# The row sums D of an attention backward as one column of products, read by VectorE as a scalar per row

## The chip, the cores and the metric

The kernel runs on one core of a Trainium2 chip. The metric is the device time of one execution in microseconds (us); the median of several runs is given. TensorE multiplies (PE in the profile's lines, its weight loads PEld), VectorE (DVE), ScalarE (ACT) and GpSimd (POOL) work element by element, and SyncE (SP) issues DMA transfers.

## The reference

Forward, a block with conditioned layer norms, a segment-recurrent attention with a memory of 8 rows, and a gated MLP; the kernel returns its output and the gradients of eleven inputs for a given `grad_out`. The attention, with 64 segments of 32 rows, 32 heads of 128 and 40 positions in each segment (8 of memory, 32 of the segment):

```
for s in range(64):
    h = concatenate([mem, x[s * 32:(s + 1) * 32]])            # 40 rows of 512
    q, k, v = h @ Wq, h @ Wk, h @ Wv                          # per head
    p = softmax(where(mask, q @ k.T * scale, -1e9))           # 40 x 40 per head
    o = (p @ v) @ Wo
    mem, out[s] = o[:8], o[8:]
```

Its backward runs from the last segment to the first, because `mem` ties each segment to the one behind it. For each head, with dO the gradient of `p @ v`:

```
dV = P.T @ dO
dP = dO @ V.T
D  = rowsum(dO * O)
dS = scale * P * (dP - D)
dQ = dS @ K;  dK = dS.T @ Q
dh = dQ @ Wq.T + dK @ Wk.T + dV @ Wv.T
```

## The kernel before

The program has stages: setup and forward attention (to about 930 us of the span), the MLP forward and backward (to about 1456 us), the backward of the attention (`phase4`, to about 2420 us), and the weight gradients of the attention (`phase5`). The change lies in `phase4` alone, a loop of 64 steps, one for each segment.

The 32 heads are laid out as 11 groups of three heads (3 x 40 = 120 rows, in columns of 128). Most steps work on all 11 groups in three batches of 4, 4 and 3 groups (`NP = 3`, `PG = 4`), one batch to a PSUM bank, since a batch is 4 x 128 float32. One step does, in the order in which it is written:

- `col_pass`: the products dO = dy Wo^T; `turn` transposes them into `dOT`; copies also make `dOst`, dO by rows.
- `grad_mm("dVT", ...)`: products for dV transposed (tile `g_ps`, line 1890); `prod(pi)`: VectorE multiplies `OT` by `dOT` in place (line 1849); `dp(pi)`: the products dP into `dp_ps` (line 1867).
- `ds(pi)`: for each group one product with a matrix of minus ones (`negones`) that adds -D to all 120 columns of dP in the same bank (line 1875). Then one VectorE instruction for the batch takes (dP - D) times `scale` times `Pst` into `dS` (line 1877).
- `dht(dVT, WvT, 0)` and `1`: the heads of dV in the products for dh (`col_mm`, line 215, four at a time in 32 columns each; 24 heads, then the last 8 later).
- `gv2`: the last batch for dV transposed; `gr0`, `gr1`, `gr2`: three batches for dV by rows, copied by `rv_out` into `rv_rows` (shown as `rows_x`), the first by ScalarE, the others by VectorE.
- `dstt(pi)`: TensorE transposes `dS` into `tps` (line 1807), a copy makes `dST`: batches 0 and 2 by ScalarE, 1 by VectorE.
- `gks`: products for dK (line 1890, `g_ps<-dS,Qst`), copied by `grad_out` into `dKT`: batch 0 by ScalarE, 1 and 2 by VectorE. Then `gq`: products for dQ (`g_ps<-dST,Kst`), copied by ScalarE into `dQT`. Behind the last copy of each, SyncE issues a transposing DMA, and GpSimd later stores the rows.
- `dht` for the 32 heads of dK and the last 8 of dV; `fold_split` takes that sum; `dht_pairs` multiplies dQ; `sum_pair` adds, and ScalarE puts the memory rows of the result into the next segment's `dyT`.

Copies go through one helper, `evac` (lines 61 and 63). At the end of the loop `pin` fixes the program's order on every engine as it is written, so nothing is reordered. Some steps have extras: every fourth step VectorE copies half of a tile `RBd` ahead of its dS instructions, another fourth ScalarE copies the other half, and in some 14 steps a small transpose from another sum (`dh_b`) stands in the place of this step's own, which comes later.

PSUM tiles of the loop with the tag `p` share a pool of six banks:

```
psp = self.psp = self.ps_ctx.enter_context(tc.tile_pool(name="p4ps", bufs=6, space=PSUM, reuse_waits="tile"))
```

When a tile is asked for, the pool picks one of the banks whose last tile has been given up in the program's order. The first product into the new tile waits for the last instruction that read the old one. Which bank a tile gets is settled when the program is built, and can change when the instructions before it do.

Of the kernel before, what the change touches and what calls it, by code (L numbers as in the profile page):

```python
# [9 lines left out]
AF = mybir.ActivationFunctionType  # L10
ALU = mybir.AluOpType
# [29 lines left out]
class K:  # L41
# [1631 lines left out]
    def phase4(self):  # L1673
        nc, tc, cfg, io = self.nc, self.tc, self.cfg, self.io
        D, DC, H, E, L, M, T, G, NS = cfg.D, cfg.DC, cfg.H, cfg.E, cfg.L, cfg.M, cfg.T, cfg.G, cfg.NS
        GW = 128
# [4 lines left out]
        with self.p4_ctx as ctx:  # L1681
            WqT, WkT, WvT, WoT, negones = self.WqT, self.WkT, self.WvT, self.WoT, self.negones
# [9 lines left out]
            PG = 4  # L1692
# [28 lines left out]
            def part3(t, pi):  # L1721
                return t[:, pi * PW:min((pi + 1) * PW, G * GW)].rearrange("p (g x) -> p g x", x=GW)
# [79 lines left out]
            def transposes_part(src, pi, w=GW, m=128):  # L1802
                ps = ps_b16("tps")
                n = min(PG, G - pi * PG)
                for j in range(n):
                    g = pi * PG + j
                    nc.tensor.transpose(ps[:, j, 0:m], src[0:m, g * w:g * w + GW], self.ident[0:m, 0:m])  # L1807
                return ps[:, 0:n, 0:m]
# [22 lines left out]
            for s in reversed(range(NS)):  # L1831
# [11 lines left out]
                VT, OT, Pst, Kst, Qst = ld["VT"], ld["OT"], ld["Pst"], Kst_t, Qst_t  # L1843
                dS, dST, dOst = dSs[0], dSTs[0], dOst_t
                dVT, dKT, dQT = dXTs["dVT"][0], dXTs["dKT"][0], dXTs["dQT"][0]
# [24 lines left out]
                def ds(pi):  # L1870
                    ps = dps[pi]
                    n = min(PG, G - pi * PG)
                    for j in range(n):
                        g = pi * PG + j
                        nc.tensor.matmul(ps[:, j, 0:120], lhsT=OT[:, g * GW:(g + 1) * GW], rhs=negones[:, 0:120],  # L1875
                                         start=False, stop=True, skip_group_check=True)
                    nc.vector.scalar_tensor_tensor(out=part3(dS, pi)[:, :, 0:120], in0=ps[:, 0:n, 0:120],  # L1877
                                                   scalar=cfg.scale, in1=part3(Pst, pi)[:, :, 0:120],
                                                   op0=ALU.mult, op1=ALU.mult)

                def grad_part(nm, lh, rh, xt, pi, eng):
                    grad_out(nm, xt, pi, eng, grad_mm(nm, lh, rh, pi))

                def grad_mm(nm, lh, rh, pi):
                    ps = ps_f32("g_ps")
                    n = min(PG, G - pi * PG)
                    for j in range(n):
                        g = pi * PG + j
                        w = GW if nm == "dV" else 120
                        nc.tensor.matmul(ps[:, j, 0:w], lhsT=lh[:, g * GW:(g + 1) * GW], rhs=rh[:, g * GW:g * GW + w],  # L1890
                                         start=True, stop=True)
                    return ps

                def grad_out(nm, xt, pi, eng, ps):
                    self.evac(eng, part3(xt, pi)[:, :, 0:120], ps[:, 0:min(PG, G - pi * PG), 0:120])
                    if pi == NP - 1 and nm != "dVT":
                        rows = rxp.tile([128, G, 128], BF16, name="rows_x")
                        nc.sync.dma_start(rows[:], xt[:, :], transpose=True)
                        dram = {"dKT": self.DKR, "dQT": self.DQR}[nm][s]
                        row_stores.append(lambda: nc.gpsimd.dma_start(dram, rows[:]))  # L1900
# [3 lines left out]
                def rv_out(pi, eng, ps):  # L1904
                    n = min(PG, G - pi * PG)
                    self.evac(eng, rv_rows[:, pi * PG:pi * PG + n, :], ps[:, 0:n, :])

                def dstt(pi):
                    ps = transposes_part(dS, pi, m=120)
                    self.evac("dve" if pi == 1 else "act", part3(dST, pi)[:, :, 0:120], ps)  # L1910
# [4 lines left out]
                def dht(X, WT, pi):  # L1915
                    if dh_ps[0] is None:
                        dh_ps[0] = psb.tile([128, 512], F32, name="dh_ps", tag="dh")
                    for h in range(pi * PG * 3, min(H, (pi + 1) * PG * 3)):
                        off = (h // 3) * GW + (h % 3) * 32
                        self.col_mm(dh_ps[0], X[:, off:off + 32], WT[:, h, :], n_dh[0], 2 * H)  # L1920
                        n_dh[0] += 1
# [35 lines left out]
                prod(2)  # L1957
                dp(2)
                grad_out("dVT", dVT, 0, "act", gv0)
                if b_done:  # L1960
                    b_done()
                dost(2)
                grad_out("dVT", dVT, 1, "act", gv1)
                ds(0)
                ds(1)
                ds(2)
                self.pop_later()
                dht(dVT, WvT, 0)
# [3 lines left out]
                gr1 = grad_mm("dV", Pst, dOst, 1)  # L1972
# [11 lines left out]
                    self.dO_tails(s - 1, RBds[((s - 1) // 4) % 2])  # L1984
                grad_out("dVT", dVT, 2, "dve", gv2)
                rv_out(0, "act", gr0)
                rv_out(1, "dve", gr1)
                dstt(0)
                dstt(1)
                dstt(2)  # L1990
                rv_out(2, "dve", gr2)
                row_stores.append(lambda s=s, rows=rv_rows: nc.gpsimd.dma_start(self.DVR[s], rows[:]))
# [5 lines left out]
                for pi in range(NP):  # L1998
# [2 lines left out]
                        load_rows(Kst_t, self.KST, s - 1)  # L2001
                    grad_out("dQT", dQT, pi, "act", gq)
                split = tail.split()
                for pi in range(NP):
                    dht(dKT, WkT, pi)
                dht(dVT, WvT, 2)
                parts = self.fold_split(sb2, dh_ps[0], "dh", dST)
                pair = self.split_pair(sb2, dht_pairs(dQT, WqT), "dh")
                tail.collect(s % nseg_t, [dVT, dKT, dQT])
# [7 lines left out]
                g = s // 4  # L2017
# [469 lines left out]
```

## Time and profile before

| What | us |
|---|---|
| median of 3 runs | 2976.55 |
| lowest and highest of them | 2974.73 to 2981.98 |
| profiled execution, its own time | 2976.49 |
| span of that execution | 2974.4 |
| a plain step of the backward loop | 14.5 |
| TensorE busy in the loop, 1456 to 2420 us | 951.87 of 964 |
| VectorE, ScalarE, GpSimd busy there | 577.77, 499.66, 447.31 |

The span is what the profile's lines add up in; the execution's own time has 2.1 us more around it. Products are pipelined and their ends are modelled, so that a busy TensorE may still have small waits between starts. In the lines of instruction groups the numbers are busy us, mean ns of one, and then the idle time of the engine just before them with what ended most of it. In the timeline each line is start, length, engine, line, operation, tiles (out<-in), shape and count, and instructions of one kind that follow each other are one line.

### The profile page before, as it was taken

The numbers are of one execution on the slowest core, as the hardware profiler recorded it, in microseconds if no ns is written. First come the engines' busy times: TensorE is split into PE (matmuls) and PEld (weight loads), VectorE is DVE, ScalarE is ACT, GpSimd is POOL, SyncE is SP. The second block draws the span as 40 slices with busy tenths as digits, with TensorE's granted clock in tenths as the row PEclk, the third lists the DMA queues.
The fourth block names the chain that finished last, engine by engine and source line by source line (L and its number), as shares of the span: only waits on it lengthen the run. The fifth ranks groups of instructions, "written<-read, shape, count | busy, mean of one in ns | idle before, by whom it ended". The sixth has DMA issues, their size and how long they took to land.

```text
span 2974.4 us, 105326 instructions
## 1 busy us (share of the span) xinstructions
PE 2905.7 (98%) x43742; PEld 1816.9 (61%) x43816; DVE 1620.3 (54%) x3683; ACT 1348.0 (45%) x3244; POOL 1233.2 (41%) x2486
## 2 busy tenths in 40 slices
PE   6999999999998999999999999999999999999999
PEld 3666666666665544445677777777777754445545
DVE  5565666656655788733456666666566532850011
ACT  3666666666665544312355555555555520110011
POOL 2555545545545222221344444444444432762111
PEclk9999999999999999999999999999999999999999
DMA  9888898988999899998699999999999997876565
GB/s 308 221 223 220 213 218 229 217 216 224 223 226 267 209 234 229 246 280 274 190 252 256 252 250 252 249 253 247 253 251 252 247 274 246 262 252 191 161 215 171
DMA packets 838066, 703.01 MB, mean 236 GB/s; under 512 B 537698, under 2 KB 710162, under 8 KB 836692
## 3 DMA queue, kind: packets, MB, share of 16 engines
q1 hardware_dynamic: 711972, 485.29, 66.3%
q0 software_dynamic: 54512, 148.63, 15.8%
q10 hardware_dynamic: 71104, 62.34, 6.5%
q8 instruction: 345, 5.65, 0.8%
q14 instruction: 133, 1.09, 0.1%
HBM read 294.99 MB, written 276.35 MB: 192 GB/s over the span
## 4 chain that ended last, share of the span: by engine, by line
PE 89%; DMA 5%; DVE 2%; issue 2%; ACT 1%; SPq 1%; POOL 1%; DVEq 0%; POOLq 0%; ACTq 0%
PE gps L2267 14%; PE pass_ps L257 14%; PE dh_ps L215 8%; PE g_ps L1890 5%; PE pass_ps L675 5%; PE gps5o L2282 4%; PE dhq_ps L223 4%; PE at_ps L223 4%; PE mm L1371 3%; PE gps L1550 3%; PE dh_tps L215 3%; PE turn_ps L880 2%; PE mm L1331 2%; PE mm L1346 2%; PE tps L1807 2%
## 5 line engine op out<-in xcount | busy, mean ns | idle before, releaser
L2267 PE MATMUL gps<-rows,hrows 128*128 128x512 bf16 (+2 forms) x2124 | 413.6, 355 | 1.9
L2267 PEld LDWEIGHTS <-hrows 128*128 128x128 bf16 x2160 | 211.1, 98 | 204.5 <-issue 0.9
L1118 POOL TENSOR_TENSOR Pst<-Pst,rden 120x1408 bf16<-120x1408 bf16 x63 | 159.7, 2535 | 315.1 <-issue 204.0
L63 DVE CAST ot<-gps 128x512 bf16<-128x512 f32 (+3 forms) x76 | 48.2, 634 | 310.8 <-PE gps L2267 229.2
L61 ACT ACTIVATE ot<-gps 128x512 bf16<-128x512 f32 (+3 forms) x75 | 41.2, 549 | 355.0 <-PE gps L2267 228.0
L1935 POOL COPY dOst<-RAd 96x512 bf16<-96x512 bf16 x128 | 75.1, 611 | 297.0 <-DVE RAd L63 297.0
L675 PE MATMUL pass_ps<-Wv,hT 128*32 128x512 bf16 (+2 forms) x2304 | 186.7, 357 | 0.0
L2271 POOL DMA_DIRECT2D out_dram<-ot x104 | 78.5, 755 | 257.6 <-DVE ot L63 133.4
L257 PEld LDWEIGHTS <-hT 128*32 128x32 bf16 x4096 | 117.0, 97 | 96.5 <-issue 6.2
L63 DVE CAST Vst<-pass_ps 96x512 bf16<-96x512 f32 x128 | 87.1, 681 | 106.5 <-ACT RBv L61 103.0
L215 PE MATMUL dh_ps<-WvT,dVT 128*32 128x512 bf16 x2048 | 133.4, 380 | 1.8 <-DVE RBd L63 0.2
L223 PE MATMUL at_ps<-Wo,OT 128*32 128x256 bf16 x4096 | 127.8, 276 | 1.2 <-ACT OT L61 1.0
L675 PE MATMUL pass_ps<-Wv,hb 128*32 128x512 bf16 (+2 forms) x636 | 126.5, 339 | 0.2 <-POOL hb L428 0.2
L257 PE MATMUL pass_ps<-Wk,hT 128*32 128x512 bf16 x2048 | 122.7, 380 | 2.1 <-POOL hT L561 1.1
L257 PE MATMUL pass_ps<-Wq,hT 128*32 128x512 bf16 x2048 | 124.1, 381 | 0.0
L257 PE MATMUL pass_ps<-WoT,dyT 128*32 128x256 bf16 (+1 forms) x3072 | 122.6, 308 | 0.9 <-ACT dyT L2016 0.9
L223 PE MATMUL dhq_ps<-WqT,dQT 128*32 128x256 bf16 x4096 | 122.9, 273 | 0.0
L215 PE MATMUL dh_ps<-WkT,dKT 128*32 128x512 bf16 x2048 | 122.3, 380 | 0.0
L2282 PE MATMUL gps5o<-WoT,rows 128*128 128x512 bf16 x549 | 120.4, 379 | 1.2 <-DMA rows<-OSR 0.6
L223 PEld LDWEIGHTS <-dQT 128*32 128x32 bf16 x4096 | 109.8, 97 | 15.7
L317 DVE TENSOR_TENSOR dST<-dh_ps,dST 128x512 bf16<-128x512 f32 x64 | 44.3, 692 | 130.0 <-ACT dST L316 130.0
L1877 DVE SCALAR_TENSOR_TENSOR dS<-dp_ps,Pst_l 128x480 bf16<-128x480 f32 (+1 forms) x192 | 106.3, 610 | 10.0 <-PE dp_ps L1875 4.1
(475 smaller groups left out, 7038.6 us busy)
## 6 DMA issues: line engine op xcount, KB each, us to landing
OSR<-Ost SPq DMA_DIRECT2D x64, 352.0 KB
OT<-OT SPq DMA_DIRECT2D x64, 352.0 KB
PS<-Pst SPq DMA_DIRECT2D x64, 352.0 KB
Pst_l<-PS SPq DMA_DIRECT2D x64, 352.0 KB
OT_l<-OT SPq DMA_DIRECT2D x64, 352.0 KB
DVR<-rows_x POOLq DMA_DIRECT2D x64, 352.0 KB, 6.3
DKR<-rows_x POOLq DMA_DIRECT2D x64, 352.0 KB, 6.1
DQR<-rows_x POOLq DMA_DIRECT2D x64, 352.0 KB, 3.2
```

What stands on the lines that cost most here:

```text
L63: return nc.vector.tensor_copy(out, in_)
L215: self.nc.tensor.matmul(ps[32 * j:32 * j + 32, :], lhsT=lhsT, rhs=w, start=(n < 4), stop=(n >= total - 4), tile_position=(0, 32 * j))
L223: nc.tensor.matmul(ps[32 * j:32 * j + 32, :], lhsT=x[k], rhs=w[k][:, 256 * d:256 * d + 256], start=(n == 0), stop=(n == total - 1), tile_p ...
L257: self.nc.tensor.matmul(ps[32 * j:32 * j + 32, :], lhsT=lhs(c), rhs=rhs, start=(c == 0), stop=(c == DC - 1), tile_position=(0, 32 * j))
L675: nc.tensor.matmul(ps[32 * j:32 * j + 32, o * E:(o + n) * E], lhsT=lhsT, rhs=wc[:, 3 * a + hl:3 * (a + n - 1) + hl + 1:3, :], start=(c == ...
L1118: nc.gpsimd.tensor_tensor(Pst[0:120, :, :], Pst[0:120, :, :], rden[:, :].unsqueeze(2).to_broadcast([120, G, 128]), op=ALU.mult)
L1371: nc.tensor.matmul(hp[:], lhsT=xT[:, fc, :], rhs=wT[:, fc, :], start=(n == 0), stop=(n == 2 * FC - 1))
L1550: nc.tensor.matmul(ps[:], lhsT=h2r[:, j, c * 128:(c + 1) * 128], rhs=xr[:, j, :], start=(j == 0), stop=(j == NT - 1))
L1877: nc.vector.scalar_tensor_tensor(out=part3(dS, pi)[:, :, 0:120], in0=ps[:, 0:n, 0:120], scalar=cfg.scale, in1=part3(Pst, pi)[:, :, 0:120], ...
L1890: nc.tensor.matmul(ps[:, j, 0:w], lhsT=lh[:, g * GW:(g + 1) * GW], rhs=rh[:, g * GW:g * GW + w], start=True, stop=True)
L2267: nc.tensor.matmul(ps[:, 0:ng * E], lhsT=hrows[:, tp_, c * 128:(c + 1) * 128], rhs=rows[:, tp_, 0:ng * E], start=(tp_ == 0), stop=(tp_ == ...
L2282: nc.tensor.matmul(pss[gg][:], lhsT=rows[:, t, gg * E:(gg + 1) * E], rhs=dyrows[:, t, :], start=(n == 0), stop=(n == NTP - 1))
```

## The change

D is formed once for each row instead of in 120 equal columns. The product with `negones` gets one column, written into column 120 of the group's 128 in dP's bank, which was not used. VectorE's one instruction for a batch becomes one for each group, 11 in a step: it reads that column as a scalar per row, adds it to dP, and multiplies by `Pst`. The factor `scale` leaves it, and stands in the copies of dK and dQ instead, which multiply by a constant.

Two lines also change place: VectorE's copy `rv_out(1)` goes behind the first two `dstt`, and the last 8 heads of dV go ahead of the 32 heads of dK in the products for dh. Instructions on TensorE, ScalarE, GpSimd and the DMA queues are as many as before; VectorE has 8 x 64 = 512 more.

```diff
                     for j in range(n):
                         g = pi * PG + j
-                        nc.tensor.matmul(ps[:, j, 0:120], lhsT=OT[:, g * GW:(g + 1) * GW], rhs=negones[:, 0:120],
+                        nc.tensor.matmul(ps[:, j, 120:121], lhsT=OT[:, g * GW:(g + 1) * GW], rhs=negones[:, 0:1],
                                          start=False, stop=True, skip_group_check=True)
-                    nc.vector.scalar_tensor_tensor(out=part3(dS, pi)[:, :, 0:120], in0=ps[:, 0:n, 0:120],
-                                                   scalar=cfg.scale, in1=part3(Pst, pi)[:, :, 0:120],
-                                                   op0=ALU.mult, op1=ALU.mult)
+                    for j in range(n):
+                        o = (pi * PG + j) * GW
+                        nc.vector.scalar_tensor_tensor(out=dS[:, o:o + 120], in0=ps[:, j, 0:120], scalar=ps[:, j, 120:121],
+                                                       in1=Pst[:, o:o + 120], op0=ALU.add, op1=ALU.mult)
...
                 def grad_out(nm, xt, pi, eng, ps):
-                    self.evac(eng, part3(xt, pi)[:, :, 0:120], ps[:, 0:min(PG, G - pi * PG), 0:120])
+                    dst, src = part3(xt, pi)[:, :, 0:120], ps[:, 0:min(PG, G - pi * PG), 0:120]
+                    if nm == "dVT":
+                        self.evac(eng, dst, src)
+                    elif eng == "act":
+                        nc.scalar.activation(dst, src, AF.Copy, scale=cfg.scale)
+                    else:
+                        nc.vector.tensor_scalar_mul(dst, src, cfg.scale)
                     if pi == NP - 1 and nm != "dVT":
...
                 grad_out("dVT", dVT, 2, "dve", gv2)
                 rv_out(0, "act", gr0)
-                rv_out(1, "dve", gr1)
                 dstt(0)
                 dstt(1)
+                rv_out(1, "dve", gr1)
                 dstt(2)
                 rv_out(2, "dve", gr2)
...
                 split = tail.split()
+                dht(dVT, WvT, 2)
                 for pi in range(NP):
                     dht(dKT, WkT, pi)
-                dht(dVT, WvT, 2)
```

## The prediction

> **What bounds the kernel now.** I read the page first, then the waits, the groups by shape, and the timeline of one step of the backward loop. The profiled execution took 2976.49 us, at the median of the runs shown (2976.55), so sums go against 2976.5; its span is 2974.4, with 2.1 us around it.
>
> ```profile
> PE 2905.7 (98%) x43742; PEld 1816.9 (61%) x43816; DVE 1620.3 (54%) x3683; ACT 1348.0 (45%) x3244; POOL 1233.2 (41%) x2486
> PE 89%; DMA 5%; DVE 2%; issue 2%; ACT 1%; SPq 1%; POOL 1%; DVEq 0%; POOLq 0%; ACTq 0%
> ```
>
> TensorE carries the chain that ended last; VectorE and ScalarE are half idle. So VectorE work counts only where TensorE comes to wait for it. The loop takes about 14.6 us a step, 64 times. The timeline of a plain step (start, length, engine, line, operation, count), other rows left out:
>
> ```profile
> 1905.33 0.98 DVE L1849 TENSOR_TENSOR OT_l<-dOT,OT_l 128x480 bf16<-128x480 bf16 x3
> 1906.04 0.74 PE L1875 MATMUL dp_ps<-negones,OT_l 128*128 128x120 bf16 x11
> 1906.45 1.66 DVE L1877 SCALAR_TENSOR_TENSOR dS<-dp_ps,Pst_l 128x480 bf16<-128x480 f32 x3
> 1906.63 0.56 ACT L61 ACTIVATE dVT<-g_ps 128x480 bf16<-128x480 f32 x1
> 1906.77 1.48 PE L215 MATMUL dh_ps<-WvT,dVT 128*32 128x512 bf16 x24
> 1908.35 0.78 PE L1890 MATMUL g_ps<-dOst,Pst_l 128*128 128x128 bf16 x11
> 1908.77 0.60 ACT L61 ACTIVATE rows_x<-g_ps 128x512 bf16<-128x512 f32 x1 [1.58 <-PE g_ps L1890]
> 1908.96 0.74 PE L1807 MATMUL tps<-ident,dS 120*128 120x120 bf16 x11
> 1909.07 0.68 DVE L63 CAST rows_x<-g_ps 128x512 bf16<-128x512 f32 x1
> 1909.37 0.93 ACT L61 ACTIVATE dST<-tps 128x480 bf16<-128x480 bf16 x2
> 1909.54 0.79 PE L1890 MATMUL g_ps<-dS,Qst 128*128 128x120 bf16 x11
> 1910.16 0.74 PE L1890 MATMUL g_ps<-dST,Kst 128*128 128x120 bf16 x11
> 1910.19 0.58 ACT L61 ACTIVATE dKT<-g_ps 128x480 bf16<-128x480 f32 x1
> 1910.84 1.91 PE L215 MATMUL dh_ps<-WkT,dKT 128*32 128x512 bf16 x32
> ```
>
> From 1908.35 to 1910.84 TensorE runs four blocks of 11 products with almost nothing between them: gr, the transposes of dS, gk, gq. Each block goes in batches of 4, 4, 3, each in one of six rotating PSUM banks. A batch of four lasts 0.21 us, ScalarE's copy of one 0.5 to 0.6. This stretch is smooth only while no batch needs a bank copied out just before.
>
> **The products for D.** Before, 11 products 120 wide start (0.74 - 0.216)/10 = 0.052 us apart. No row shows one column; the nearest is 32 columns, after it the groups of L1877 and scalar operands used below (busy, mean ns):
>
> ```profile
> L242 PE MATMUL dh_ft<-foldsel,dh_hi 128*128 128x32 bf16 x256 | 16.8, 179 | 2.0 <-ACT dh_hi L230 2.0
> L1877 DVE SCALAR_TENSOR_TENSOR dS<-dp_ps,Pst_l 128x480 bf16<-128x480 f32 x128 | 78.2, 653 | 10.0 <-PE dp_ps L1875 4.1
> L1877 DVE SCALAR_TENSOR_TENSOR dS<-dp_ps,Pst_l 128x360 bf16<-128x360 f32 x64 | 33.6, 524 | 0.0
> L1386 DVE SCALAR_TENSOR_TENSOR junk<-dxh,xh 128x512 f32<-128x512 f32 x15 | 10.2, 681 | 0.0
> L1393 DVE SCALAR_TENSOR_TENSOR ta<-dxh,rstd,Wk 128x512 f32<-128x512 f32 x8 | 5.9, 743 | 0.0
> ```
>
> In the timeline four 32-wide products end 0.27 us after the first starts, so they start (0.27 - 0.18)/3 = 0.03 apart. The bounds are 0.052 (nothing saved) and 0.03; I take 0.03, the narrow row: 11 x 0.022 = 0.24 us. Not all of it arrives. The last three products need the last OT*dOT product (L1849, done at 1906.31), so start at 1906.36 rather than 1906.46, 0.05 being the lag from a copy's end to the product waiting for it (below). The dVT heads start at 1906.60, not 1906.77. Their second dozen needs ScalarE's dVT copy, done at 1906.63 + 0.56 = 1907.19; with 0.04 to the weight load and 0.09 to the product that is 1907.32, against 1907.42 now. So TensorE gains 0.10 us in a plain step; 0.02 in the 16 steps where ScalarE also copies half of RBd and dVT is 0.08 later; nothing in some 14 where VectorE copies the other half, for which these heads wait. About 0.06 x 64 = 4 us.
>
> **VectorE.** Three instructions a step become eleven. The rows give (653 - 524)/120 = 1.08 ns per element, so 120 elements cost 653 - 360 x 1.08 = 266 ns; the scalar read per row adds 743 - 681 = 62: 328 ns. Three now take 1.66 us where their lengths add to 1.83, so each overlaps the next by 0.085. Eleven starting d apart end 10 d + 0.33 after the first: d is 0.19 if the scalar is fetched under cover (266 - 85, rounded up), 0.24 with it, 0.33 with no overlap. I take 0.24: 2.7 us against 1.66. Starting at 1906.34 they end at 1909.1, not 1908.1. [...]
>
> **The moved copy.** rv_out(1) (0.68 us, VectorE) goes behind VectorE's dST copy (0.40). VectorE then ends the dST copy at about 1910.05, rv_out(1) at 1910.65, rv_out(2) 1911.1, dKT 1911.7 and 1912.1. Putting the 8 last dVT heads first costs nothing and gives the dKT copies 2 x 0.216 = 0.43 us more room.
>
> **The scale** in the dK and dQ copies: the same instruction with a constant, at the copies' 0.52 to 0.60 us. Bounds nothing to the 62 ns above on each; I take nothing. No DMA is added; those of dK and dQ are issued from the same copies.
>
> **The banks.** Here the sum is decided. In the built program of the changed kernel, in nearly every step, the first batch of dS transposes gets the bank that held the first batch of gr, and so waits for ScalarE's copy of it; before, that bank came from VectorE's last dS instruction, long done. The first gk batch then waits for ScalarE's dST copy of that very transpose batch; before, it waited for the gr copy. The second gq batch waits for ScalarE's dKT copy of the first gk batch (in some 14 steps with one more small transpose, the first gq batch does). So four batches pass through one bank, each behind a ScalarE copy:
> - gr's first batch starts its last product at 1908.52, less 0.10 gained: 1908.42. ScalarE starts 0.25 later (1908.77 now), 0.60: 1909.27; with the lag, transposes at 1909.32. The lag of 0.05: gk takes 0.79 where gq takes 0.74, because its second batch waits for rv_out(1), which ends at 1909.75.
> - last transpose of the batch +0.16, +0.25 to ScalarE, +0.57, +0.05: gk at 1910.35 (now 1909.54).
> - again +0.16 +0.25 +0.58 +0.05: second gq batch at 1911.39. Between lie two gk batches and one gq batch, 11 x 0.0525 = 0.58, so 0.25 is left as waiting.
> - two gq batches (0.21 + 0.105 to the last start) and 0.146 to the next heads: 1911.85, against 1910.84 now.
>
> That is 1.0 us later in a plain step: waits of 0.45, 0.45 and 0.25 less the 0.10 gained and the 0.05 that goes. It is 1.08 in the 16 steps and about 1.09 in the 14. VectorE's dST (1910.05), rv_out(1) (1910.65) and dKT copies are in time at d = 0.24. After the heads everything follows TensorE, so nothing takes the delay up. Sum: 34 x 1.0 + 16 x 1.08 + 14 x 1.09 = 66.5 us, 2976.5 + 66.5 = **3043 us**.
>
> **Rivals.**
> 1. VectorE becomes the bound. From d = 0.28 its eleventh instruction ends after 1909.4 and the second transpose batch waits for it. At 0.33 it ends at 1909.97; through dST and dKT the second gq batch falls 0.21 later, 0.4 in the 14 steps: 50 x 0.21 + 14 x 0.4 = 16 us more, 3059. For it: no row shows a scalar read from PSUM. Against: the overlap in the present rows.
> 2. One-column products as dear as 120-wide ones: the 4 us gain is gone, 3047. Then the change does not do what it says for TensorE. The 32-wide row speaks against it.
> 3. The other side: the delay is taken up downstream. If the heads behind gq (4.1 us to the next ScalarE split) had 1.0 us of slack against something that is not behind TensorE, only the saving in products would be left, at most 11 x 0.022 x 64 = 15 us: 2961. It decides from 1.0 us of such slack a step. A few steps do wait for a DMA (the longest 1.5 us), but the other waits (0.4 for RAd, 0.4 for dh_hi) hang on TensorE's own products, so they move along.
>
> **How the numbers follow.** The forecast has 0.76, rival 1 0.12, rival 2 0.05, rival 3 0.07, of which 0.02 is for a delay taken up just so far that the time stays. A measurement here tells about 0.3% (9 us) from no change. The way from a batch through its copy to the next is good to 0.1 us at worst; over three copies and 64 steps that is 19 us either way. The low end 3022 is that; the high end 3066 holds rival 1 and most of the same spread. Faster 0.05, same 0.02, slower 0.93.
>
> **What would show it.** In the timeline after: the transposes 0.4 to 0.5 us behind the last gr product, TensorE waiting for ScalarE's rows_x and dST copies some 25 to 30 us each over the loop, gq split by about 0.25 us, TensorE's busy time lower while the loop takes some 15.6 us a step. The L1879 group would show about 330 ns each and 2.7 us for eleven. I am wrong if the transposes follow gr without a gap, or if their releaser is VectorE's dS.

## The result, and the profile after

The changed kernel takes 3036.9 us (median of 5 runs, 3035.35 to 3045.68) where the kernel before takes 2974.73 (5 runs, 2971.65 to 2981.98): a ratio of 1.0216, with a 95% interval of 1.0203 to 1.023. The forecast was 3043 us in a range of 3022 to 3066. The profiled execution took 3036.07 us, 59.6 more than the profiled one of before.

The page of the changed kernel, engines and chain. TensorE's share of the chain falls from 89% to 82%; ScalarE's rises from 1% to 3%, "issue", time in which an engine waited for nothing that the profile shows, from 2% to 6%:

```profile
PE 2927.0 (96%) x43816; PEld 1802.2 (59%) x43816; DVE 1695.6 (56%) x4195; ACT 1359.9 (45%) x3244; POOL 1231.3 (41%) x2486
PE 82%; issue 6%; ACT 3%; POOL 2%; DMA 2%; DVE 2%; POOLq 0%; DVEq 0%; SPq 0%; ACTq 0%
```

The timeline of a plain step (start, length, engine, line, operation, count; the bracket is idle time and what ended it):

```profile
1934.06 0.55 PE L1875 MATMUL dp_ps<-negones,OT_l 128*128 128x1 bf16 x11
1934.34 2.89 DVE L1879 SCALAR_TENSOR_TENSOR dS<-dp_ps,Pst_l 128x120 bf16<-128x120 f32 x11
1934.62 1.48 PE L215 MATMUL dh_ps<-WvT,dVT 128*32 128x512 bf16 x24
1936.20 0.78 PE L1891 MATMUL g_ps<-dOst,Pst_l 128*128 128x128 bf16 x11
1936.62 0.60 ACT L61 ACTIVATE rows_x<-g_ps 128x512 bf16<-128x512 f32 x1 [1.41 <-PE g_ps L1891]
1937.27 0.74 PE L1807 MATMUL tps<-ident,dS 120*128 120x120 bf16 x11 [0.29 <-ACT rows_x L61]
1937.68 0.93 ACT L61 ACTIVATE dST<-tps 128x480 bf16<-128x480 bf16 x2 [0.46 <-PE tps L1807]
1938.21 1.15 DVE L63 CAST rows_x<-g_ps 128x512 bf16<-128x512 f32 x2
1938.30 0.74 PE L1891 MATMUL g_ps<-dS,Qst 128*128 128x120 bf16 x11 [0.29 <-ACT dST L61]
1938.76 0.57 ACT L1900 ACTIVATE dKT<-g_ps 128x480 bf16<-128x480 f32 x1
1938.88 1.03 PE L1891 MATMUL g_ps<-dST,Kst 128*128 128x120 bf16 x11
1939.84 0.61 PE L215 MATMUL dh_ps<-WvT,dVT 128*32 128x512 bf16 x8
```

From D's first product to the heads is 1939.84 - 1934.06 = 5.78 us; before it was 1910.84 - 1906.04 = 4.80. TensorE stands still where ScalarE's copies end: 0.60 after 1936.62 gives 1937.22, and the transposes start at 1937.27; the gk block starts at 1938.30, 0.05 behind the first of the two dST copies (0.57 long, so done at 1938.25); the gq block lasts 1.03 instead of 0.74, for its second batch waits for ScalarE's dKT copy (done at 1939.33; that batch starts at 1939.38). The waits over the loop name the same copies (time in all, times, longest). They count less than the gaps between starts (0.29 against 0.45), because a product's modelled end lies 0.16 behind the next one's place to start (0.215 long, 0.052 from start to start). So the third line has only the 14 steps in which the first gq batch waits; in a plain step the gap of 0.29 leaves an idle time of 0.13, which the list does not show:

```profile
PE tps L1807 <- ACT rows_x L61: 18.5, 63, 0.3
PE g_ps L1891 <- ACT dST L61: 18.3, 63, 0.3
PE g_ps L1891 <- ACT dKT L1900: 4.0, 14, 0.3
```

From the first product for D of the loop to that of its last step is 998.46 us against 934.79 before, 63.7 more for 63 steps, whose mean is 15.85 us against 14.84. By the trace a plain step went from 14.55 to 15.54, one in which ScalarE copies half of RBd from 14.67 to 15.73, one with the other transpose from 15.33 to 16.46. From there to the end nothing moved (577.0 us against 577.6); the loop began 3.5 us earlier in this execution, behind stages that the change does not touch, and the profiled executions of this document scatter by 9 us there.

The groups of VectorE and TensorE that the change made (busy, mean ns):

```profile
L1879 DVE SCALAR_TENSOR_TENSOR dS<-dp_ps,Pst_l 128x120 bf16<-128x120 f32 x704 | 184.8, 338 | 2.9 <-PE dp_ps L1875 2.4
L1875 PE MATMUL dp_ps<-negones,OT_l 128*128 128x1 bf16 x704 | 34.4, 165 | 0.4 <-issue 0.4
```

### The profile page after: what moved, and what is told of

Same layout as the page of the kernel before. It is cut to its first block, busy times and chain, and to the rows that moved or that the text cites. A ratio compares the mean times of both kernels' runs of the same rounds, so it can differ in the third digit from the quotient of the medians.

```text
span 3034.0 us, 105848 instructions
## 1 busy us (share of the span) xinstructions
PE 2927.0 (96%) x43816; PEld 1802.2 (59%) x43816; DVE 1695.6 (56%) x4195; ACT 1359.9 (45%) x3244; POOL 1231.3 (41%) x2486
## 4 chain that ended last, share of the span: by engine, by line
PE 82%; issue 6%; ACT 3%; POOL 2%; DMA 2%; DVE 2%; POOLq 0%; DVEq 0%; SPq 0%; ACTq 0%
PE gps L2274 14%; PE pass_ps L257 12%; PE dh_ps L215 7%; PE pass_ps L675 5%; PE gps5o L2289 4%; PE dhq_ps L223 4%; PE at_ps L223 4%; PE mm L1371 3%; PE dh_tps L215 3%; PE gps L1550 3%; PE g_ps L1891 3%; PE turn_ps L880 2%; PE mm L1331 2%; PE mm L1346 2%; PE st_ps L890 1%
## 5 line engine op out<-in xcount | busy, mean ns | idle before, releaser
L1879 DVE SCALAR_TENSOR_TENSOR dS<-dp_ps,Pst_l 128x120 bf16<-128x120 f32 x704 | 184.8, 338 | 2.9 <-PE dp_ps L1875 2.4
```

The costliest lines, as they stand in the source:

```text
L1879: nc.vector.scalar_tensor_tensor(out=dS[:, o:o + 120], in0=ps[:, j, 0:120], scalar=ps[:, j, 120:121], in1=Pst[:, o:o + 120], op0=ALU.add, ...
```

## The experiments

The theory under test: the loss is TensorE waiting for PSUM banks that ScalarE has just to copy out. Its rivals: VectorE's longer dS, the two moved steps, the scale in the copies. All ratios are to the kernel before, in runs on the same chip, with a 95% interval in brackets. The experiments ran in two rounds, each with its own runs of the kernel before: a median of 2977.72 us for the bank handed on, the moves undone, the moves alone and the scale, and of 2980.03 us for the others. Differences in us are against these.

**The bank handed on, and nothing else.** The kernel before, with one tile used four times by hand (the first gk batch and the second gq batch get `gr0` as their tile in the same way):

```diff
                 def dstt(pi):
-                    ps = transposes_part(dS, pi, m=120)
+                    if pi == 0:
+                        ps = gr0[:].rearrange("p a b -> p (a b)").bitcast(BF16)[:, 0:PG * GW].rearrange("p (a b) -> p a b", b=GW)
...
-                gks = [grad_mm("dKT", Qst, dS, pi) for pi in range(NP)]
+                gks = [grad_mm("dKT", Qst, dS, pi, gr0 if pi == 0 else None) for pi in range(NP)]
...
-                    gq = grad_mm("dQT", Kst, dST, pi)
+                    gq = grad_mm("dQT", Kst, dST, pi, gr0 if pi == 1 else None)
```

> The kernel before, whose VectorE work, products and order are kept; only one bank is passed on by hand: the first transposes of dS, the first gk batch and the second gq batch are written into the tile of gr's first batch. Theory: the three waits for ScalarE's copies come back without any change on VectorE: 0.46, 0.45 and 0.25 us less 0.05 in a plain step, 0.89 in the 14 others, in all +68 us, about 3043. Rival (VectorE's longer dS makes the loss): 2975, no change.

Measured 3043.7 us, ratio 1.0223 (1.0206 to 1.0241), 66 us over the kernel before. Its timeline shows VectorE's three dS instructions as short as ever and the same two stops, and gq again takes 1.03:

```profile
1938.64 1.66 DVE L1877 SCALAR_TENSOR_TENSOR dS<-dp_ps,Pst_l 128x480 bf16<-128x480 f32 x3
1940.96 0.60 ACT L61 ACTIVATE rows_x<-g_ps 128x512 bf16<-128x512 f32 x1 [1.58 <-PE g_ps L1890]
1941.61 0.37 PE L1912 MATMUL g_ps<-ident,dS 120*128 120x120 bf16 x4 [0.29 <-ACT rows_x L61]
1942.64 0.74 PE L1890 MATMUL g_ps<-dS,Qst 128*128 128x120 bf16 x11 [0.29 <-ACT dST L61]
1943.21 1.03 PE L1890 MATMUL g_ps<-dST,Kst 128*128 128x120 bf16 x11
```

Handing one bank along is enough for a loss as large as the whole, with no change on VectorE.

**The banks of before given back to the changed kernel.** The two moves are undone as well, as that order goes with those banks:

```diff
                 def dstt(pi):
-                    ps = transposes_part(dS, pi, m=120)
+                    if pi == 1:
+                        ps = transposes_part(dS, pi, m=120)
+                    else:
+                        ps, n = as_b16(dps[2] if pi == 0 else gv2), min(PG, G - pi * PG)
...
-                gks = [grad_mm("dKT", Qst, dS, pi) for pi in range(NP)]
+                gks = [grad_mm("dKT", Qst, dS, pi, (gr0, gr1, dps[2])[pi]) for pi in range(NP)]
```

> The changed kernel with the two moves undone and the banks of the kernel before given back by hand: first transposes into the tile of the last dP batch, last transposes into that of gv2, gk into those of gr0, gr1 and the first transposes. The waits for ScalarE's rows_x and dST copies then go. Theory: now VectorE is late: dS ends 2.9 us after the first of D, its copy for dVT holds the last transposes to 3.8 us after D, rv_out(1) the second gk batch to 4.4 us; heads 0.67 us later than in the kernel before, against 0.98 in the changed kernel: +45 us over before, about 3021. If the bank order alone made the loss, it would be near 2972; if it made no part of it, 3037.

Measured 3019.28 us, ratio 1.0135 (1.0115 to 1.0154): 39 us over before, where the changed kernel was 62 over. The heads stand 5.43 us behind D's first product (1947.12 - 1941.69). TensorE's longest wait in the loop has a new name, VectorE's dS (the timeline, then the wait over the loop):

```profile
1941.97 2.89 DVE L1879 SCALAR_TENSOR_TENSOR dS<-dp_ps,Pst_l 128x120 bf16<-128x120 f32 x11
1944.92 0.37 PE L1925 MATMUL dp_ps<-ident,dS 120*128 120x120 bf16 x4 [0.31 <-DVE dS L1879]
1945.35 0.68 DVE L63 CAST rows_x<-g_ps 128x512 bf16<-128x512 f32 x1
1946.29 0.32 PE L1891 MATMUL dp_ps<-dS,Qst 128*128 128x120 bf16 x3
1947.12 0.83 PE L215 MATMUL dh_ps<-WkT,dKT 128*32 128x512 bf16 x12
PE dp_ps L1925 <- DVE dS L1879: 20.5, 62, 1.0
```

dS ends at 1944.86 and the transposes start at 1944.92. So the bank hand-off is what the changed kernel waits for, but taking it away recovers only a third: VectorE's late dS and the copies queued behind it stand next (its dVT copy ends at 1945.43 and the last transposes start at 1945.49; its rows_x copy ends at 1946.03 and the weight loads of the second gk batch go on at 1946.09). The two causes overlap in time, so their prices (66 us and 39 us, each alone) do not add up.

**The moves undone alone.** The diff's two moves are taken back, the rest of the change stays.

> The changed kernel with the two moves undone (D in one column, eleven VectorE instructions, scale in the copies; rv_out(1) and the heads where they were before). In the build the first transposes still take the bank of gr's first batch, the first gk batch that of the transposes, the second gq batch that of gk. Theory: the same as the changed kernel, 3037 give or take 4. Rival (the moves make the loss): some 27 us less, 3010.

Measured 3040.2 us, ratio 1.0208 (1.0193 to 1.0223), and a plain step of 15.53 us against 15.54. Taking the moves out of the changed kernel wins nothing.

**The moves alone**, in the kernel before:

```diff
                 rv_out(0, "act", gr0)
-                rv_out(1, "dve", gr1)
                 dstt(0)
                 dstt(1)
+                rv_out(1, "dve", gr1)
...
+                dht(dVT, WvT, 2)
                 for pi in range(NP):
                     dht(dKT, WkT, pi)
-                dht(dVT, WvT, 2)
```

> The kernel before with the two moves alone (rv_out(1) behind the first two transposes, the last dV heads first). The pool then gives the second gk batch the bank of the first transpose batch and the second gq batch that of the first gk batch. Theory: two waits for ScalarE of about 0.25 us a step, less the 0.05 that goes: +0.43 x 64 = +27 us, about 3002. Rival (the moves are free, as the forecast had them, and only the bank of the first transpose batch matters): 2975.

Measured 3013.18 us, ratio 1.0116 (1.0101 to 1.0131): 35 us. The heads come 0.44 us later in a plain step, as expected, and each kind of step is 0.42 to 0.45 us longer where nothing else disturbs it: some 28 us in all. The rest, in the profiled execution, is single waits of up to 2.0 us in some twenty steps, in different places of the step, most of the longer ones put down to "issue"; what makes those was not settled. With VectorE's three instructions this order costs by itself. In the changed kernel the same waits stand with the moves and without (for rows_x 18.5 and 18.4 us over the loop, for dST 18.3 in both), so there it costs nothing more.

**Only the heads moved**: the last 8 dV heads ahead, no other edit.

> The kernel before with one edit: the last 8 dV heads ahead of the 32 dK heads in the products for dh. Theory: the dK copies are in time already (dKT ends 1911.53, its heads start 1912.28), so nothing changes: 2975 give or take 3. Rival (the dK copies of VectorE hold the heads in some steps): up to 0.2 us a step, 12 us faster.

Measured 2979.25 us, ratio 1.0000 (0.9987 to 1.0013), heads at 4.79 us in place of 4.80. That move is free, so by difference the 35 us above come with the move of rv_out(1), which was not run alone.

**The scale alone**, in the copies of dK and dQ:

```diff
-                                                   scalar=cfg.scale, in1=part3(Pst, pi)[:, :, 0:120],
+                                                   scalar=1.0, in1=part3(Pst, pi)[:, :, 0:120],
...
+                    elif eng == "act":
+                        nc.scalar.activation(dst, src, AF.Copy, scale=cfg.scale)
+                    else:
+                        nc.vector.tensor_scalar_mul(dst, src, cfg.scale)
```

> The kernel before with the softmax scale alone moved into the copies of dK and dQ (D still 120 columns, VectorE's three dS instructions with the constant 1). Theory (TensorE waits for banks that ScalarE empties): no change, 2975 us give or take 3; the dK and dQ copies keep 0.52 to 0.60 us each. A rival by which the scaled copies are dearer: 62 ns more on each of six copies, at most 0.12 us a step on the path, +8 us.

Measured 2975.56 us, ratio 0.9993 (0.9984 to 1.0003): no difference that can be told. The copies with the factor keep their 590, 507, 649 and 523 ns.

**Eleven instructions without the scalar per row**:

```diff
-                    nc.vector.scalar_tensor_tensor(out=part3(dS, pi)[:, :, 0:120], in0=ps[:, 0:n, 0:120],
-                                                   scalar=cfg.scale, in1=part3(Pst, pi)[:, :, 0:120],
-                                                   op0=ALU.mult, op1=ALU.mult)
+                    for j in range(n):
+                        o = (pi * PG + j) * GW
+                        nc.vector.scalar_tensor_tensor(out=dS[:, o:o + 120], in0=ps[:, j, 0:120], scalar=cfg.scale,
+                                                       in1=Pst[:, o:o + 120], op0=ALU.mult, op1=ALU.mult)
```

> The kernel before (D in 120 columns, constant scale, no moves) with VectorE's three dS instructions a step cut into eleven. It measures the price of the cut without the scalar read per row: by the rows of before 266 ns each and 0.185 from start to start, so 2.1 us for eleven against 1.66; the changed kernel showed 338 ns and 0.255. Theory: the pool hands on other banks here (second gk batch behind ScalarE's dST copy, the last transposes behind the gr copy), waits of about 0.25 us a plain step: +16 us, about 2993. Rival (the loss goes with the number of VectorE instructions, wherever the banks are): most of the 60 us, above 3020.

Measured 3001.13 us, ratio 1.007 (1.0052 to 1.0088), 21 us; a plain step costs 0.24 more. Cutting the instruction in eleven does not bring the 60 us, and what it does bring lies again in banks. In a plain step the last transposes start 0.05 us behind ScalarE's rows_x copy, the second gk batch 0.05 behind its first dST copy, and the last gq batch 0.05 behind its dKT copy; the three blocks last 0.78, 0.95 and 0.78 us where they lasted 0.74, 0.79 and 0.74:

```profile
1936.86 0.60 ACT L61 ACTIVATE rows_x<-g_ps 128x512 bf16<-128x512 f32 x1 [1.58 <-PE g_ps L1891]
1937.05 0.78 PE L1807 MATMUL tps<-ident,dS 120*128 120x120 bf16 x11
1937.46 0.93 ACT L61 ACTIVATE dST<-tps 128x480 bf16<-128x480 bf16 x2
1937.66 0.95 PE L1891 MATMUL g_ps<-dS,Qst 128*128 128x120 bf16 x11
1938.44 0.78 PE L1891 MATMUL g_ps<-dST,Kst 128*128 128x120 bf16 x11
```

Against the changed kernel's 338 ns it gives the price of the scalar read per row (there the first operation is also an add in place of a multiply, which no run separates):

```profile
L1879 DVE SCALAR_TENSOR_TENSOR dS<-dp_ps,Pst_l 128x120 bf16<-128x120 f32 x704 | 139.0, 271 | 9.5 <-PE dp_ps L1875 3.7
```

That is 67 ns, and it is not hidden: eleven take 2.17 us here and 2.89 in the changed kernel, so from start to start (2.17 - 0.27)/10 = 0.19 and (2.89 - 0.34)/10 = 0.255.

**The gain alone**: D in one column, nothing else. The kernel then leaves the row sums out of dS, so it is of use for its time only.

```diff
-                        nc.tensor.matmul(ps[:, j, 0:120], lhsT=OT[:, g * GW:(g + 1) * GW], rhs=negones[:, 0:120],
+                        nc.tensor.matmul(ps[:, j, 120:121], lhsT=OT[:, g * GW:(g + 1) * GW], rhs=negones[:, 0:1],
```

> The kernel before with the products for D one column wide and nothing else; the row sums are then left out of dS. It measures the gain term alone. Theory: products some 0.03 us apart instead of 0.052, dVT heads 0.17 us earlier, of which ScalarE's dVT copy leaves 0.10 to 0.16 and VectorE's rv_out(1) copy, which the second gk batch waits for, takes back a little: 0.07 to 0.15 us in 34 plain steps, less in the others, 3 to 6 us faster, about 2973. Rival (a one-column product costs as much as a wide one): no change at all in the start of the dVT heads.

Measured 2975.86 us, ratio 0.999 (0.9976 to 1.0004): too little to tell in the whole time. In the steps it is plain: 14.38 us against 14.55, 14.59 against 14.67, and nothing (15.33) in the third kind, where the heads wait for VectorE's RBd copy (13 waits, 3.8 us in all). From D's first product in the loop to the last step's it is 2.3 us; one single wait of 2.8 us ahead of a `turn` product, put down to "issue", took back part of it. So even had VectorE's work been free, an estimate of 7 us was to be won (34 steps at 0.17 and 15 at 0.08).

## Why the prediction was right

- **The banks.** The first transposes behind ScalarE's gr copy, gk behind its dST copy, gq split by the dKT copy: all three show, at 0.45, 0.45 and 0.29 us, and the heads come 0.98 us later where 1.0 was forecast. The closeness is in part luck: gq's wait is 0.04 longer than forecast, since ScalarE's dKT copy starts 0.30 us behind the last product of its batch and not 0.25, and the gain of the next point is 0.07 larger, which partly cancels it. Per kind of step 1.0, 1.08 and 1.09 were forecast, and 0.99, 1.06 and 1.13 came. The loop lost 63.7 us for 66.5; most of the rest between 3043 and 3036 is the 3.5 us by which the loop began earlier. The bank handed on by hand shows that this mechanism suffices.
- **The signs.** The transposes stand 0.45 us behind gr and their releaser is ScalarE's rows_x copy, as named. Two signs came otherwise. The waits for rows_x and dST are listed at 18.5 and 18.3 us, not 25 to 30, for the list counts from modelled ends; and TensorE's busy time in the loop did not fall, it rose from 926.31 to 942.51 us. For the same reason each of the three stops in a step counts 0.16 us as busy, 0.48 in all, against the 0.17 saved in the products and the 0.05 of the wait that goes. The 14.6 and 15.6 us a step are those of a plain step; the means are 14.84 and 15.85.
- **The products for D.** They start 0.025 us apart, below the 0.03 taken from the 32-wide row, and the third batch starts 0.32 us behind the first, as worked out from the OT*dOT product. The term was still too small: the gain in a plain step is 0.17, not 0.10, because ScalarE's copy holds the weight loads of the second dozen of dVT heads (they start at 1935.27, after 0.31 of idle time), but not its products. The 0.04 + 0.09 from a copy's end to the product was too long here: the 24 heads run in 1.48 us without a gap although the copy ends (1934.65 + 0.56 = 1935.21) only 0.07 us before the second dozen starts (1935.28).
- **VectorE.** 338 ns and 2.89 us for 328 and 2.7; d is 0.255, close to the forecast's middle value. It is in time only because the bank waits cover it. The forecast named the price beyond d = 0.28 and not what VectorE would cost if the banks were mended: 39 us, by the run with the banks of before given back.
- **The moves** were costed at nothing. In the changed kernel that holds, by the run with the moves undone; by themselves, in the kernel before, they cost 35 us.
- **The scale** at nothing is right, and so is the heads' move. None of the rivals came: d stayed under 0.28, the narrow products are cheap (0.025 us apart), and no slack downstream takes the delay up (from the heads to the next D a plain step takes 9.76 us before and after).

## What to carry to other kernels

Before an instruction is cut into more and shorter ones off the critical engine, look which PSUM banks come free when, and which batch will be written next into each: here a batch of 0.2 us behind a copy of 0.6 stopped TensorE for 0.45 us, though VectorE and ScalarE were about half idle (busy 56% and 45% of the span). When a pool chooses the banks at build time, read its choice from the built program after every edit: here one copy put behind two others cost 35 us, and three instructions cut into eleven 21 us, most of it waits for ScalarE's copies. A saving counts only up to the next thing that is late: here TensorE could win 0.17 us in a step, and VectorE had to be 1.2 us longer for it.

## What the runs showed of the hardware

With a scalar per row read from PSUM, and an add for the first multiply, VectorE's 128x120 instruction took 67 ns more (338 against 271), and all but a few ns of it showed in the distance from one start to the next (0.255 against 0.19 us). A 128x120 dS instruction with a constant took 271 ns where 480 columns took 653; from start to start the small ones were 0.19 us apart, 0.76 for four, and the wide ones 0.57. One-column products with a new 128x128 weight load each started 0.025 us apart within a batch, against 0.052 for 120 columns.
